# A gated mix of a long convolution and a shift MLP: the convolution in one piece, and in two channel chunks

## The chip, the cores and the metric

The kernel runs on one core of a Trainium2 chip. The metric is the device time of one execution in microseconds (us), lower is better. The core has five engines with an instruction queue each: PE multiplies matrices (PEld is its weight load), DVE and ACT do elementwise work and are the only ones that read PE's results out of PSUM, POOL does small elementwise work, and SP only issues transfers. SP, ACT and POOL each have a DMA queue; all of them share 16 DMA engines.

## The reference

The input is a sequence of S = 2048 rows with D = 640 channels, all in bf16. Two branches read it and a gate mixes them.

```
def _A_ref(q, k, v, shift_k, ssm_k, ssm_D):        # branch A: convolution over the sequence
    k_shift[s] = sum over t of k[s - t] * shift_k[:, t]        # 4 taps per channel
    kv = k_shift * v
    y  = causal convolution of kv with ssm_k, per channel, 2048 taps (by FFT), + kv * ssm_D
    return q * y

def _B_ref(x, w1, w2, w3, w4):                     # branch B: mixer
    h  = gelu(layernorm(x) @ w1)                   # 640 x 640
    hs = (four channel groups of h, shifted by 1, -1, 2, -2 rows) @ w2
    x1 = x + hs
    return x1 + gelu(layernorm(x1) @ w3) @ w4      # 640 x 1536, 1536 x 640

g = sigmoid((x * gate_w).sum(-1)) ; out = g * a + (1 - g) * b      # x is A_q
```

## The kernel before, in words

The sequence is laid out as 128 partitions x 16 row tiles of 640 channels; tile u holds rows 16p + u. Four tiles make a group. Q holds A_q and is later overwritten with branch B's sums.

**Branch B.** `norm_stats` takes means and variances on DVE, and 1/sqrt on POOL; `norm_apply` normalizes on DVE (xn, L329), transposes on PE (L336) and copies the transposed block XNT out of PSUM on ACT. `first_product` (L370) gives gelu(.. @ w1) into GS with the shift; `second_product` (L452) adds .. @ w2 to Q; `third_product` (L466) gives gelu(.. @ w3) into three tiles G; `fourth_product` (L479) adds .. @ w4. `US` is the order of the four tile groups in the later products.

**Branch A.** `short_conv` (L431) does the four taps on DVE: eleven elementwise operations for a group of four tiles. The long convolution is a transform in two steps. `step1` (L286) multiplies the filter's rows, then the signal's, by F1, copies the result AR out of PSUM on ACT and writes it to DRAM (SH, SX). `spectrum` (L563) goes over 32 frequency tiles t: `spec_h` reads SH back as BH, multiplies by M2 and copies to HS on ACT, and swaps the two halves of HS by two DMAs per pair of t on SP's queue; `spec_x` does the same for SX and multiplies with both forms of HS on DVE into XPB; `spec_z` multiplies by G1 and G2, copies ZG out (ACT and DVE in turn) and writes it to DRAM (SZ). `y_group` (L591) reads SZ back as ZT, multiplies by F1T, scales by the gate (ty), multiplies by q and adds branch B. The gate itself is `gate_dot` and `gate_act` on DVE and ACT; `scale_b` multiplies branch B's tile by 1 - g on ACT. `filter_transpose` (L308) turns the filter rows HN on PE and stores them as HTA (12 tiles, copied by DVE) and HTB (4 tiles, by ACT). Tables M2, G1, G2, F1 and F1T are made at the start from integers on POOL, DVE and ACT (`pbits`, `affine`, `wrap`, `sines`); `masked_blocks` spreads them into masked copies, six on ACT and six on DVE.

**Buffers.** Tiles with one tag share a ring of buffers, and a new tile waits until the oldest use of a buffer is over.

```
def big(name, ...):     tag="b5",  bufs=11      # L75: KT VT acc tmp CJ KHALO AR HTB BH BX HS ZG ZT, 5 KB each
def weights(...):       tag="w",   bufs=3       # L84: W12, GEN, HTA, W3, W4, XPB
load_h:                 tag="g",   bufs=3       # L112: HN, and later G of third_product
XNT and load_cjr's CJR: tag="xnt", bufs=2       # L325, L405
ps_tile:                tags "pc" and "pm", two PSUM buffers each
```

**Order.** Up to `front.__exit__` the engines' order is written out by hand (from the constants to the last part of `first_product(3, ..)`, with `filter_transpose` 0 to 4 and the first steps of `short_conv(0)` in between). After it a scheduler orders the instructions by the order of the program text and by when it thinks they are ready. That order is made by generators: `merge(a, b, ratio)` steps b by ratio times the cost that a yields. `conv_front` (the short convolution with step 1 of filter and signal) is merged with `mixer` at 1.0, `spectrum` with the rest of `mixer` at 1.5; then come the third product of the last group, `y_group` 3 and 0, and the last fourth product merged with `y_group` 1 and 2. The spectrum can start only when step 1 of all signal groups is done, since BX reads rows of all of them. Engines issue in order: an instruction that waits holds up those behind it in its queue, and a DMA on SP's queue does so too.

Of the kernel before, what the change touches and what calls it, by code (L numbers as in the profile page):

```python
# [10 lines left out]
ALU = mybir.AluOpType  # L11
# [6 lines left out]
def kernel(  # L18
# [32 lines left out]
    assert S == 2048 and P == 128 and D % P == 0 and Fh % (4 * P) == 0  # L51
# [7 lines left out]
    shifts = [1, -1, 2, -2]  # L59

# [14 lines left out]
    def big(name, shape=None, dtype=BF16):  # L75
        return main.tile(shape or [P, 4, D], dtype, name=name, tag="b5", bufs=11)
# [18 lines left out]
    def halves(ap):  # L95
        return ap.rearrange("p (h d) -> p h d", d=HD)

# [25 lines left out]
    load_h(0)  # L123
# [12 lines left out]
    def load_w2():  # L136
# [6 lines left out]
    ET = mybir.EngineType  # L143
    front = tc.manual_schedule(engines={ET.PE, ET.DVE, ET.Activation, ET.Pool})
    front.__enter__()
    IDB = consts.tile([P, P], BF16, name="IDB")
    nc.gpsimd.memset(IDB[:], 0.0)
    nc.gpsimd.affine_select(out=IDB[:], in_=IDB[:], compare_op=ALU.not_equal, fill=1.0,
                            base=0, pattern=[[-1, P]], channel_multiplier=1)
# [5 lines left out]
    def pbits(mask, mul, add, name):  # L155
        ti = consts.tile([P, 1], I32, name=name + "i")
        nc.vector.tensor_scalar(out=ti[:], in0=pidx[:], scalar1=mask, scalar2=None, op0=ALU.bitwise_and)
        tf = consts.tile([P, 1], F32, name=name)
        nc.vector.tensor_scalar(out=tf[:], in0=ti[:], scalar1=float(mul), scalar2=float(add),
                                op0=ALU.mult, op1=ALU.add)  # L160
        return tf

    pf = consts.tile([P, 1], F32, name="pf")
    nc.vector.tensor_copy(out=pf[:], in_=pidx[:])

    pf4 = pbits(31, 16, 1, "pf4")
    pfi = pbits(96, 0.125, 0, "pfi")
    nc.vector.tensor_tensor(out=pf4[:], in0=pf4[:], in1=pfi[:], op=ALU.add)

    GENW = main.tile([P, 3, 1024], I32, name="GEN", tag="w", bufs=3)  # L170


    def norm_stats(src):
        mv = small.tile([P, 4, 2], F32, name="mv")
        for i in range(4):
            st = small.tile([P, 2, 6], F32, name="st")
            for h in range(2):
                nc.vector.bn_stats(out=st[:, h, :], in_=src[i][:, h * HD:(h + 1) * HD])  # L178
            nc.vector.bn_aggr(out=mv[:, i, :], in_=st[:])
        ve = small.tile([P, 4], F32, name="ve")  # L180
        nc.gpsimd.tensor_scalar(out=ve[:], in0=mv[:, :, 1], scalar1=1e-5, scalar2=None, op0=ALU.add)
        rs = small.tile([P, 4], F32, name="rs")
        nc.gpsimd.tensor_tensor(out=rs[:], in0=ve[:], in1=NH[:], op=ALU.pow)
        return mv, rs
# [3 lines left out]


    F1 = consts.tile([P, 2, P], BF16, name="F1")  # L190
    F1T = consts.tile([P, 2, P], BF16, name="F1T")
    for gi, (dst, col_mul, col_add, prow) in enumerate(((F1, 4, 1, pf), (F1T, 1, 0, pf4))):
        t1 = main.tile([P, 320], I32, name="GENF", tag="r", bufs=6)
        t2 = main.tile([P, 320], I32, name="GENF", tag="r", bufs=6)
        ic = t1[:, 0:P]
        nc.gpsimd.iota(ic, pattern=[[col_mul, P]], base=col_add, channel_multiplier=0)
        jj = t2[:, 0:2 * P].rearrange("p (c k) -> p c k", c=2)
        for comp, off in ((0, 384.0), (1, 0.0)):
            nc.vector.tensor_scalar(out=jj[:, comp, :], in0=ic, scalar1=prow[:], scalar2=off,
                                    op0=ALU.mult, op1=ALU.add)  # L200
        last_f = nc.vector.tensor_scalar(out=jj, in0=jj, scalar1=511, scalar2=None, op0=ALU.bitwise_and)
        nc.scalar.activation(out=dst[:], in_=jj, func=ACT.Sin, bias=NPI[:], scale=2 * PI_ / 512)
# [7 lines left out]
    GA, GB, GC = GENW[:, 0, :], GENW[:, 1, :], GENW[:, 2, :]  # L210
    icf, ick, icn, m1 = GA[:, 0:512], GA[:, 512:1024], GB[:, 0:512], GB[:, 512:1024].bitcast(F32)
    nc.gpsimd.iota(icf.rearrange("p (g i n) -> p g i n", i=4, n=16), pattern=[[64, 8], [4, 4], [512, 16]],
                   base=0, channel_multiplier=0)
    nc.gpsimd.iota(ick.rearrange("p (g i n) -> p g i n", i=4, n=16), pattern=[[64, 8], [4, 4], [0, 16]],
                   base=0, channel_multiplier=0)
    nc.gpsimd.iota(icn.rearrange("p (m n) -> p m n", n=16), pattern=[[0, KH], [1, 16]],
                   base=0, channel_multiplier=0)
    midp = pbits(120, 0.125, 0, "midp")
    basep = pbits(3, 16, 1, "basep")
    offp = [pbits(4, -512, 6144 + 2048 * ro, f"offp{ro}") for ro in range(2)]  # L220
    for ro in range(2):
        nc.vector.scalar_tensor_tensor(out=offp[ro][:], in0=basep[:], scalar=midp[:], in1=offp[ro][:],
                                       op0=ALU.mult, op1=ALU.add)
    basei = pbits(15, 512, 1, "basei")
    kli = pbits(48, 0.0625, 0, "kli")
    nc.vector.scalar_tensor_tensor(out=basei[:], in0=kli[:], scalar=16.0, in1=basei[:], op0=ALU.mult, op1=ALU.add)
    offi = [pbits(64, -64, 6144 - 2048 * o, f"offi{o}") for o in range(2)]
    off2 = consts.tile([P, 1], F32, name="off2")
    nc.vector.memset(off2[:], 6144.0)
# [13 lines left out]

    for ro in range(2):
        affine(GC[:, 512 * ro:512 * ro + 512], icf, midp[:], offp[ro][:])
    st0 = norm_stats(tiles_of(range(4)))
    nc.vector.scalar_tensor_tensor(out=m1, in0=ick, scalar=basei[:], in1=icn, op0=ALU.add, op1=ALU.mult)
    wrap(GC)
    for o in range(2):
        affine(GA[:, 512 * o:512 * o + 512], m1, 1.0, offi[o][:])  # L250
    sines(M2, GC, True)
    for o in range(2):
        affine(GC[:, 512 * o:512 * o + 512], m1, 1.0, (0.0, off2[:])[o])
    klf = pbits(3, 1, 0, "klf")
    MK = []
    for name, kl in (("f", klf), ("i", kli)):
        mk = consts.tile([P, 4], F32, name="mk" + name)
        MK.append(mk)

    def masks():  # L260
        for mk, kl in zip(MK, (klf, kli)):
            for j in range(4):
                nc.vector.tensor_scalar(out=mk[:, j:j + 1], in0=kl[:], scalar1=float(j), scalar2=None,
                                        op0=ALU.is_equal)

    def masked_blocks():
        n = 0
        for dst, mk, inner in ((M2, MK[0], True), (G1, MK[1], False), (G2, MK[1], False)):
            for j in range(4):
# [9 lines left out]
                yield 0.0  # L279


    SH = dram.tile([32, P, D], BF16, name="SH")
    SX = dram.tile([32, P, D], BF16, name="SX")
    SZ = dram.tile([4, 32, 32, D], BF16, name="SZ")

    def step1(src, dst_dram, g):  # L286

        for hf in range(2):
            AR = big("AR", [P, 2, 2, D])
            for n in range(2):  # L290
                for h in range(2):
                    c0 = (2 * hf + n) * D + h * HD
                    ps = ps_tile("ps1", "pc")
                    for comp in range(2):
                        nc.tensor.matmul(ps[:, comp, 0:HD], lhsT=F1[:, comp, :], rhs=src[:, c0:c0 + HD],  # L295
                                         start=True, stop=True)
                    evac("a", AR[:, n, :, h * HD:(h + 1) * HD], ps[:, :, 0:HD])
                    yield 0.27
            r0 = 8 * g + 4 * hf
            nc.scalar.dma_start(out=bass.AP(tensor=dst_dram.tensor, offset=dst_dram[r0, 0, 0].offset,  # L300
                                            ap=[[D, P], [P * D, 4], [1, D]]),
                                in_=AR[:].rearrange("p n r d -> p (n r) d"))


    HT, HTA = [], []
    held = {}

    def filter_transpose(dt):  # L308
        if not HT:
            hta = weights("HTA", [P, 12, D])  # L310
            HTA.append(hta)
            HT.extend([hta[:, 4 * g:4 * g + 4] for g in range(3)] + [big("HTB")[:]])
        pst = psum.tile([P, N2, P], BF16, name="psh", tag="pc")
        hv = HN[dt].rearrange("p (n m) -> p n m", m=N2)
        for n2 in range(N2):
            nc.tensor.transpose(out=pst[:, n2, :], in_=hv[:, :, n2], identity=IDB[:])
        held["v"] = evac("v", HTA[0][:, :, dt * P:(dt + 1) * P], pst[:, 0:12, :])
        held["a"] = evac("a", HT[3][:, :, dt * P:(dt + 1) * P], pst[:, 12:16, :])
        if dt == DT - 1:
            nc.vector.tensor_tensor(out=HT[0][0:1, 0, :], in0=HT[0][0:1, 0, :], in1=DROW[0:1, :], op=ALU.add)  # L320
# [497 lines left out]
```

## Time and profile before

| what | value |
|---|---|
| median of 3 runs | 314.17 us (311.94 to 315.86) |
| the profiled execution, its own time | 313.56 us |
| its span in the profile | 311.8 us |
| mean granted TensorE clock | 0.949 |
| instructions | 4270 |
| DMA | 59.59 MB in 28,087 packets, 191 GB/s mean |
| DMA engines' busy share by queue | SP 37.7%, ACT 15.9%, POOL 3.5% |

The profile is of one execution. Busy time is the sum of an engine's instructions; a wait is put down to what came last before the waiting instruction could start; the chain follows the end of the execution back from step to step. L numbers are lines of the kernel. "DMA X<-Y" as a releaser is a transfer from Y to X. A line such as L90 is that of a helper (`evac` on ACT; L93 the same on DVE), so its tiles' names tell what it is.

### The profile page before, as it was taken

The page shows a single profiled execution, that of the slowest core. Times are in us where ns is not written, and L with a number is a line of the kernel's source. Part 1 is how long each engine was busy: PE and PEld are TensorE (multiplying, and loading weights), DVE is VectorE, ACT ScalarE, POOL GpSimd, SP SyncE. Part 2 cuts the span into 40 slices and gives each one's busy share as a digit, 9 for nine tenths or more (in the row PEclk, how much of TensorE's full clock was granted, in tenths as well). Part 3 has the DMA queues.
Part 4 walks back from the last instruction along what each step waited for, and adds up shares of the span by engine and source line. Part 5 has one row for each costly group of instructions (what it writes and reads, how often), then busy time and mean ns, then how long its engine had stood idle before and what let it go on. Part 6 is the DMA issues. An engine that isn't in the chain of part 4 may idle for free.

```text
span 311.8 us, 4270 instructions
## 1 busy us (share of the span) xinstructions
PE 246.6 (79%) x1572; PEld 148.1 (48%) x1572; DVE 198.5 (64%) x411; ACT 186.7 (60%) x265; POOL 38.1 (12%) x72
## 2 busy tenths in 40 slices
PE   0266729795986972899999883999998997599994
PEld 0223406563642440466447552665555664345673
DVE  8887805299985910499908893799443565601982
ACT  4493432426986686283685271467889799546740
POOL 4555450225010000000000320000000000000000
PEclk9997969999996998699999997899999999999999
DMA  7992771000275259442844797668774945269741
GB/s 227 396 254 103 253 321 67 2 17 6 86 247 205 93 188 373 159 170 84 273 149 133 215 326 253 211 192 225 261 229 140 291 146 161 89 220 371 263 182 63
DMA packets 28087, 59.59 MB, mean 191 GB/s; under 512 B 2051, under 2 KB 19203, under 8 KB 28066
## 3 DMA queue, kind: packets, MB, share of 16 engines
q1 hardware_dynamic: 13042, 38.18, 37.7%
q10 hardware_dynamic: 14224, 17.70, 15.9%
q0 software_dynamic: 800, 3.44, 3.5%
q8 instruction: 12, 0.20, 0.3%
q14 instruction: 9, 0.07, 0.1%
HBM read 35.71 MB, written 18.35 MB: 173 GB/s over the span
## 4 chain that ended last, share of the span: by engine, by line
PE 53%; DVE 22%; DMA 10%; ACT 8%; POOL 3%; issue 3%; SPq 0%; ACTq 0%; POOLq 0%; DVEq 0%
PE psw L479 16%; PE psw L466 14%; DVE st L178 5%; PE psz L542 5%; DMA W<-in_B_w_dram 4%; PE psw L452 4%; DMA BX<-SX 4%; PE psw L370 3%; ACT XNT L90 3%; PE psy L603 3%; PE ps L295 3%; PE psx L526 2%; DVE acc L441 2%; DVE tmp L439 2%; PE psh L513 2%
## 5 line engine op out<-in xcount | busy, mean ns | idle before, releaser
L479 PE MATMUL psw<-W,G 128*128 128x320 bf16 x384 | 64.7, 308 | 8.3 <-DMA W<-in_B_w_dram 6.4
L466 PE MATMUL psw<-XNT,W 128*128 128x512 bf16 x240 | 60.6, 387 | 0.2 <-ACT G L363 0.2
L90 ACT CAST AR<-ps 128x640 bf16<-128x640 f32 x64 | 41.5, 701 | 25.5 <-PE ps L295 20.1
L479 PEld LDWEIGHTS <-G 128*128 128x128 bf16 x384 | 38.6, 101 | 25.2 <-DMA W<-in_B_w_dram 6.8
L531 DVE TENSOR_TENSOR XPB<-XPB,HS 128x640 bf16<-128x640 bf16 x64 | 28.3, 487 | 21.3 <-ACT XPB L90 21.3
L466 PEld LDWEIGHTS <-W 128*128 128x128 bf16 x240 | 23.9, 99 | 24.0 <-issue 2.2
L363 ACT ACTIVATE G<-psw 128x1024 bf16<-128x1024 f32 x24 | 24.9, 1038 | 11.0 <-PE psw L466 10.9
L91 ACT ACTIVATE HS<-psh 128x640 bf16<-128x640 f32 x32 | 22.8, 719 | 13.1 <-PE psh L513 13.1
L370 PE MATMUL psw<-XNT,W 128*128 128x512 bf16 x80 | 21.7, 425 | 10.5 <-ACT XNT L90 9.6
L336 PE MATMUL pst<-IDB,xn 128*128 128x128 bf16 x160 | 13.6, 231 | 18.2 <-POOL GS L348 13.8
L90 ACT CAST XPB<-psx 128x640 bf16<-128x640 f32 x32 | 22.6, 707 | 8.9 <-PE psx L526 8.8
L542 PE MATMUL psz<-XPB,G 128*128 128x320 bf16 x128 | 23.6, 303 | 5.0 <-DVE ZG L93 1.6
L90 ACT COPY XNT<-pst 128x2048 bf16<-128x2048 bf16 (+1 forms) x16 | 19.3, 1240 | 13.6 <-PE pst L336 7.1
L178 DVE BATCH_NORM_STATS2 st<-Q 128x6 f32<-128x320 bf16 x64 | 27.3, 466 | 0.1
L452 PE MATMUL psw<-W,GS 128*128 128x320 bf16 x160 | 23.8, 299 | 4.1 <-ACT XNT L90 2.9
L455 DVE TENSOR_TENSOR Q<-psw,Q 128x640 bf16<-128x640 f32 x16 | 12.8, 806 | 14.5 <-PE psw L452 14.5
L295 PEld LDWEIGHTS <-F 128*128 128x128 bf16 x128 | 12.5, 98 | 19.4 <-issue 12.5
L336 PEld LDWEIGHTS <-xn 128*128 128x128 bf16 x160 | 11.0, 103 | 21.6 <-DVE xn L329 17.8
L452 PEld LDWEIGHTS <-GS 128*128 128x128 bf16 x160 | 15.6, 98 | 10.8 <-issue 4.8
L370 PEld LDWEIGHTS <-W 128*128 128x128 bf16 x80 | 8.7, 108 | 22.0 <-issue 15.2
L526 PE MATMUL psx<-BX,M 128*128 128x320 bf16 x64 | 14.5, 308 | 5.8 <-DMA BX<-SX 4.9
L542 PEld LDWEIGHTS <-G 128*128 128x128 bf16 x128 | 12.4, 98 | 13.8 <-issue 6.9
(113 smaller groups left out, 344.3 us busy)
## 6 DMA issues: line engine op xcount, KB each, us to landing
SH<-AR ACTq DMA_DIRECT2D x8, 640.0 KB, 3.6
SX<-AR ACTq DMA_DIRECT2D x8, 640.0 KB, 3.3
BH<-SH SPq DMA_DIRECT2D x8, 640.0 KB, 4.3
HS<-HS SPq DMA_DIRECT2D x32, 160.0 KB, 2.9
BX<-SX SPq DMA_DIRECT2D x8, 640.0 KB, 4.4
SZ<-ZG ACTq DMA_DIRECT2D x8, 640.0 KB, 3.4
ZT<-SZ SPq DMA_DIRECT2D x8, 640.0 KB, 6.2
HN<-in_A_ssm_k_dram SPq DMA_DIRECT2D x5, 512.0 KB, 10.9
```

The source lines that it names most:

```text
L90: return nc.scalar.copy(out=o, in_=i)
L91: return nc.scalar.activation(out=o, in_=i, func=ACT.Copy, scale=scale)
L178: nc.vector.bn_stats(out=st[:, h, :], in_=src[i][:, h * HD:(h + 1) * HD])
L295: nc.tensor.matmul(ps[:, comp, 0:HD], lhsT=F1[:, comp, :], rhs=src[:, c0:c0 + HD], start=True, stop=True)
L336: nc.tensor.transpose(out=pst[:, dd, i * P:(i + 1) * P], in_=xns[i][:, (d0 + dd) * P:(d0 + dd + 1) * P], identity=IDB[:])
L363: nc.scalar.activation(out=o, in_=i, func=ACT.Gelu_apprx_tanh)
L370: nc.tensor.matmul(ps[:, j, :], lhsT=w1_cols(dt, nt), rhs=XNT[:, dt, :], start=(dt == 0), stop=(dt == DT - 1))
L452: nc.tensor.matmul(ps[:, h, 0:HD], lhsT=GS[:, nt, u, :], rhs=W2P[:, nt, h * HD:(h + 1) * HD], start=(nt == 0), stop=(nt == DT - 1))
L466: nc.tensor.matmul(ps[:, j, :], lhsT=W3[:, dt, (f + j) * P:(f + j + 1) * P], rhs=XNT[:, dt, :], start=(dt == 0), stop=(dt == DT - 1))
L479: nc.tensor.matmul(ps[:, h, 0:HD], lhsT=G[ft // 4][:, ft % 4, i * P:(i + 1) * P], rhs=W4[0][:, ft, h * HD:(h + 1) * HD], start=(ft == 0), ...
L531: nc.vector.tensor_tensor(out=xp[:, 1 + a, :], in0=xp[:, 0, :], in1=HS[t // 2][:, a, t % 2, :], op=ALU.mult)
L542: mm = nc.tensor.matmul(pz[:, h, 0:HD], lhsT=gm[:, t].rearrange("p a b c -> p (a b c)"), rhs=XP[t][:, 1 + a, h * HD:(h + 1) * HD], start=( ...
```

## The change

The long and the short convolution are done in two chunks of channels, c = 0 with 384 and c = 1 with 256; all of KT, VT, KHALO, CJ, AR, BH, BX, HS, ZG, ZT and the DRAM buffers SH, SX, SZ exist per chunk. `big` becomes `chunk`, 18 buffers of 3 KB. `CJR` moves from the "xnt" ring into it, and taps are loaded and split per chunk. The spectrum's loop goes over 16 pairs m of frequency tiles: one PSUM tile holds both tiles of a pair, the product with both forms of HS is one DVE instruction on a tile PQ of the chunk ring, and XPB is gone. Two pairs of `spec_h` run ahead (before, five single tiles).

The order is now: `conv_a` (chunk 0: short convolution, step 1) with the mixer at 1.1; `spectrum(0)` with `conv_b` (chunk 1) at 2.2 and the mixer at 3.0; `spectrum(1)` with `mixer_end` at 1.4, which is the fourth product of US[2] and the y groups of chunk 0; then the third product of the last group, y of chunk 1 for groups 3 and 0, and the last fourth product with y of chunk 1 for groups 1 and 2. The 16 gate dots are woven into the fourth product of US[1] and the third of US[2], and every `scale_b` is issued in `y_group`.

In the front, the constants are made by three DVE operations on a row of eleven columns that POOL fills with memsets, instead of two operations per constant; GEN lies in the "g" ring as three tiles, so all loads of HN come after the sines; F1T is made after the sines; the memset of KHALO goes from POOL to DVE; `bn_aggr` is issued one tile later than its `bn_stats`; only three filter transposes and the first two steps of chunk 0's `short_conv(0, 0)` are in it. Transfers of K, V and the output are by chunk: 768 or 512 bytes per row and tile.

The diff, cut to its core:

```diff
-    def big(name, shape=None, dtype=BF16):
-        return main.tile(shape or [P, 4, D], dtype, name=name, tag="b5", bufs=11)
+    CH = [(0, DA * P), (DA * P, D - DA * P)]
+    def chunk(name, shape):
+        return main.tile(shape, BF16, name=name, tag="b3", bufs=18)
+    def pair(name, w):
+        return main.tile([P, 2, w], BF16, name=name, tag="xs", bufs=3)
...
+    def weave(lead, *others):
+        owed = [0.0] * len(others)
+        for c_ in lead:
+            yield c_
+            for n, (g_, speed) in enumerate(others):
+                owed[n] += c_ * speed
+                while owed[n] > 0:
+                    got = next(g_, None)
+                    if got is None:
+                        break
+                    owed[n] -= got
...
-    GENW = main.tile([P, 3, 1024], I32, name="GEN", tag="w", bufs=3)
+    GEN = [main.tile([P, 1024], I32, name="GEN", tag="g", bufs=3) for _ in range(3)]
...
+    const_row(cm[:, 0, :], cmask)
+    const_row(ca[:, 0, :], cmul)
+    const_row(ca[:, 1, :], cadd)
...
+    def step1(src, dst, g, w):
+        for hf in range(2):
+            AR = chunk("AR", [P, 2, 2, w])
+            for n in range(2):
+                ps = ps_tile("ps1", "pc")
+                for comp in range(2):
+                    nc.tensor.matmul(ps[:, comp, 0:w], lhsT=F1[:, comp, :], rhs=src(2 * hf + n),
+                                     start=True, stop=True)
+                evac("a", AR[:, n, :, :], ps[:, :, 0:w])
...
-        cjr = main.tile([P, D, 4], BF16, name="CJR", tag="xnt", bufs=2)
-        nc.gpsimd.dma_start(out=cjr[:], in_=A_shift_k.partition_broadcast(P))
+        cjr = chunk("CJR", [P, w, 4])
+        nc.gpsimd.dma_start(out=cjr[:], in_=A_shift_k[c0:c0 + w, :].partition_broadcast(P))
+        cj = chunk("CJ", [P, 4, w])
...
-        nc.gpsimd.memset(t[0:1, :, :], 0.0)
+        t = chunk("KHALO", [P, 3, w])
+        nc.vector.memset(t[0:1, :, :], 0.0)
...
+    def spec_x(c, m):
+        w = CH[c][1]
+        ps = forward(BX[c, m // 2], m, w)
+        xs = pair("XS", w)
+        evac("a", xs[:], ps[:, :, 0:w])
+        pq = chunk("PQ", [P, 2, 2 * w])
+        nc.vector.tensor_tensor(out=pq[:], in0=xs[:].rearrange("p t d -> p (t d)").unsqueeze(1).to_broadcast([P, 2, 2 * w]),
+                                in1=HS[c, m][:].rearrange("p a t d -> p a (t d)"), op=ALU.mult)
...
+    def spectrum(c):
...
+        for m in range(AH):
+            spec_h(c, m)
+            yield 0.33 * u
+        spec_x(c, 0)
+        yield 0.33 * u
+        for m in range(NM):
...
+            if m + AH < NM:
+                spec_h(c, m + AH)
+            if m + 1 < NM:
+                spec_x(c, m + 1)
+            yield 0.66 * u
+            spec_z(c, m)
+            yield 0.66 * u
...
+    def conv_b():
+        w = CH[1][1]
+        load_h(3)
+        load_h(4)
+        cjr = load_cj(1)
+        split_cj(1, cjr)
+        load_halo(1)
+        load_kv(1, 0)
+        load_kv(1, 1)
+        filter_transpose(3)
+        yield 1.0
+        filter_transpose(4)
+        yield 1.0
...
-    merge(conv_front(rows), mix, 1.0)
-    XPB.append(weights("XPB", [P, 4, 3, D]))
-    merge(spectrum(), mix, 1.5)
-    run(mix)
+    mix, conv = mixer(), conv_b()
+    run(weave(conv_a(), [mix, 1.1]))
+    run(weave(spectrum(0), [conv, 2.2], [mix, 3.0]))
+    run(conv, mix)
+    def mixer_end():
+        ya = chain(*[y_group(0, g) for g in range(NG)])
+        for i, u in enumerate(US[2]):
+            with tc.issue_after(LAST[-1].ins):
+                run(fourth_product([u], G_[2], False, i))
+            yield 3.2
+            for _ in range(2 if i < 3 else 1):
+                yield next(ya)
+        yield from ya
+    mix = mixer_end()
+    run(weave(spectrum(1), [mix, 1.4]))
+    run(mix)
     with tc.issue_after(LAST[-1].ins):
         run(third_product(Ys[0], G_[3]))
-    early = set(US[3])
-    run(y_group(3, early), y_group(0, early))
-    merge(fourth_product(US[3], G_[3], True), chain(y_group(1, early), y_group(2, early)), 0.6)
+    run(*[y_group(1, g) for g in (3, 0)])
+    run(weave(fourth_product(US[3], G_[3], True), [chain(y_group(1, 1), y_group(1, 2)), 0.6]))
```

## The prediction

> **What bounds the kernel now.** I read the page first, then busy time by stretch, then the chain that ended last, then the waits and the forms of the instructions.
>
> ```profile
> PE 246.6 (79%) x1572; PEld 148.1 (48%) x1572; DVE 198.5 (64%) x411; ACT 186.7 (60%) x265; POOL 38.1 (12%) x72
> ```
> ```profile
> 0.00:78.40 78.40, 45.82 (x326) 27.21 (x327) 53.52 (x148) 36.58 (x53) 31.86 (x62) 0.93 0.49 164
> 78.40:272.30 193.90, 165.35 (x1027) 99.63 (x1027) 127.43 (x228) 131.58 (x190) 6.28 (x10) 0.95 0.61 197
> 272.30:311.80 39.50, 35.39 (x221) 21.30 (x218) 17.57 (x37) 18.57 (x23) 0.00 (x0) 0.98 0.59 217
> ```
> The columns are PE, PEld, DVE, ACT and POOL busy, granted clock, DMA share, GB/s. The cuts are mine: 78.4 is where the second product of US[1] starts on PE, 272.3 where the spectrum ends. No engine is full: the front waits on a chain through all engines, the middle has PE at 85% with DVE and ACT at 66% and 68%, and only the tail is PE's own.
>
> The chain, in order of time (start, length, what):
> ```profile
> 40.35 2.78 POOL CJ L412 x4
> 43.16 1.88 ACT XNT L90
> ...
> 91.78 4.42 DMA SH<-AR
> ...
> 114.17 11.67 DMA W<-in_B_w_dram
> ...
> 182.29 11.20 DMA BX<-SX
> ...
> 272.32 12.95 PE psw L466 x60
> ```
> The waits (total, times, longest):
> ```profile
> DVE acc L438 <- DMA SH<-AR: 17.2, 1, 17.2
> ...
> ACT XNT L90 <- POOL CJ L412: 6.4, 1, 6.4
> ...
> PE psw L479 <- DMA W<-in_B_w_dram: 6.4, 1, 6.4
> ```
> X2's XNT sits in a two-slot ring, one slot of which CJR holds until POOL has split it. The short convolution of group 1 stops 17.2 us because AR holds the slots of the 11-buffer ring that acc needs. W4 waits for HTA's slot.
>
> One instruction shows a neighbour's cost (timeline, start and length):
> ```profile
> 21.75 1.69 POOL L419 MEMSET KHALO<- 1x1920 bf16 x1
> 21.83 3.33 DVE L329 TENSOR_SCALAR xn<-Q,mv,rs 128x640 bf16<-128x640 bf16 x4 [1.12 <-POOL rs L183]
> ...
> 33.29 1.51 DVE L329 TENSOR_SCALAR xn<-Q,mv,rs 128x640 bf16<-128x640 bf16 x4
> ```
>
> **Prices.** PE at full clock: 12.95/60 = 0.216 us for 512 columns and, from the tail's 6.53 us for 48, 0.136 for 320; so 0.163 for 384 and 0.109 for 256. ACT out of PSUM has rows of 0.384 (256 columns), 0.490 (384), 0.600 (512), 0.70 (640), 1.04 (1024); 768 is 0.81 between the last two. DVE on bf16: 1.49 us for 2560 elements, 28.3/64 = 0.44 for 640, so 0.09 plus 0.55 ns each. DVE out of PSUM: 0.82 for 640.
>
> **Front (78.4 us).** CJR leaves XNT's ring: ACT's 6.4 us go. What is late next is st3's rs, ready at 40.35, whose user X3 starts only at 53.2, so I take all of it (ends 5 and 6.4). KHALO's memset moves from POOL to DVE: four xn cost 1.8 us less; the memset on one partition costs DVE between 0.06 (the NPI memset) and 1.69 (this one on POOL); nearer DVE's own row, 0.4: gain 1.4. From 62.3 to 81 the chain is DVE's work. Two of three HTA copies leave it (1.9 us), the DROW add narrows by 0.3, and the nine conv0 pieces there, 9.4 us, become 0.81 + 0.6 × 8.6 = 6.0 at 384 of 640 columns, 3.4 less: 5.6 (ends 3, if PE's first product binds instead, and 8). The tables: 2.5 us of small DVE instructions ahead of st0 shrink, but three wraps and F1T's matrix (2.1 + 1.2 us) now stand ahead of st1: zero (ends -2.7 and +2). POOL's 27 memsets are hidden by the wait for Q and st0; without that cover they cost at most 27 × 0.1 = 2.7. HN's loads move behind the sines, since GEN holds their ring, SP's W2 goes ahead of them, and the first transpose is at 31: zero, up to 3. Front: 78.4 - 6.4 - 1.4 - 5.6 = 65.0.
>
> **Middle.** The matmul columns stay the same; fixed costs shift a little. It now has three stages, and I sum each engine in each.
>
> *A, first chunk's convolution beside the mixer.* Its lead costs of about 31, times 1.1, reach half of fourth_product(US[0]). ACT: 32 AR × 0.81 = 25.9, 6 gelu 6.2, two XNT 5.0, six masked blocks 7.0: 44.1. DVE: one group is 32 × 384 × 0.55 ns + 11 × 0.09 = 7.8 us, 3.63 groups are left: 28.3; with stats 4.2, xn 3.6, adds 4.8, masks 2.8: 43.7. PE: 5.4 + 13.0 + 10.4 + 2.6 + 6.5 = 37.9. ACT leads. ACT's fullest 20 us before had 17.43 busy (87%): 44.1/0.87 = 50.7. Eighteen smaller buffers leave ten for AR beside the eight of the convolution, where there were two: the 17.2 us wait should go. W4's slot comes free after 16 AR instead of 32, so W4 should land as the third product ends: zero (ends 0 and 11.7).
>
> *B, spectrum of the first chunk, convolution of the second, the mixer's rest.* PE: fourth 6.5 + 13, second 10.8, third 26, transposes 4.9, step 1 64 × 0.109 = 7.0, spectrum 128 × 0.163 = 20.9: 89.1. DVE: four groups of 5.5 = 22, 16 products of 1536 elements at 0.93 = 14.9, gate 12.6, adds 11, ZG 7.8, stats 8.4, xn 3.6, HTB 2: 82. ACT: 26.2 + 6.6 + 19.2 + 12.5 + 5 + 1.6 = 71. PE leads as from 200 to 260 before, where it was busy 58.44 of 60 (97%): 91.9. XPB's wait for W12 goes, and nothing replaces it. A wait is added: HN 3 and 4 need slots that G_[0] holds until the fourth product of US[0] ends, and behind them on SP stand the second chunk's halo and K, V loads, the next HS swaps and BX; spec_x's product waits for those. Zero if the scheduler puts the swaps first, else up to 11.2, the length of BX's worst landing. At B's start BX reads what A's last AR wrote, 3.3 + 4.4 us by their rows; ready mixer work covers it, else it costs 7.7.
>
> *C, spectrum of the second chunk, fourth_product(US[2]), y of the first.* ACT: HS and XS 32 × 0.60 = 19.2, ZG 4.8, 16 ty × 0.49 = 7.8, 16 scale_b × 0.854 = 13.7: 45.5. PE: 14 + 13 + 5.2 = 32. DVE 29. ACT leads; the 13.7 of scale_b wait for almost nothing and fill gaps, so 0.95: 47.9.
>
> **Tail.** Third 13.0, fourth 13.0, y of 256 columns 32 × 0.109 = 3.5, so 30 for the 35.3 that PE took (272.3 to 307.6); 4.2 to the end as before.
>
> Sum: 65.0 + 50.7 + 91.9 + 47.9 + 30 + 4.2 = 289.7 of span; the execution's time was 1.8 above its span (313.56 to 311.8): 291.5, against 313.56. The median of the runs shown, 314.17, is 0.6 above that execution, well inside their spread.
>
> **Queues.** SP issues 64 HS swaps for 32 at 0.56 us each, and twice the BH, BX, ZT, K, V reads: some 70 us of SP in 290, hidden as long as a swap is issued within C's 3 us per pair (two swaps, and half of a BH and BX each, take 1.7); without that cover each pair runs later by what is over.
>
> **Packets, a price the trace lacks.** Rows of 1280 B become 768 and 512, K and V lose their 5120 B runs: SH, SX, SZ 12,288 more packets, ZT 4,096, K and V 7,168, BH, BX and HS 4,096, together 27,600. Below end: nothing, since the SP queue's packets (2927 B mean) took 37.7% of 16 × 311.8 us for 38.18 MB, 49 us of engine time per MB, and ACT's (1244 B) 15.9% for 17.70 MB, 45, no dearer when smaller. Above: every packet costs ACT's mean of 56 ns whatever its size, 27,600 × 56/16 = 97 us of all engines. I take zero, by the two rows.
>
> SH<-AR landed its 640 KB in 3.6 us. The Trainium skill (DMA: Bandwidth & Descriptors, Anatomy of one DMA, fitted there for POOL's queue) has 2.0 us fixed plus bytes over 436 GB/s, 3.5 us for that, and its Rules for kernel authors ask for 1 MiB per DMA, which speaks against this change. By it a hand-off in chunks pays 2.0 us more wherever one is waited for; at the start of each spectrum that would be 4 us, and the sum 295.5.
>
> **Rivals.** *PE all through.* If the three stages blend, only PE's columns count: (37.9 + 89.1 + 32)/0.97 = 164, and 65 + 164 + 34.2 + 1.8 = 265. For it: PE, DVE and ACT totals of the middle are alike (159, 155, 161), so an even mix could do it. Against it: ACT leads at both ends by data order.
>
> *The waits only move.* The middle stays at 85% of its leading engine: (44.1 + 89.1 + 45.5)/0.85 = 210, 311 in all. For it: 18 slots serve two convolution chunks and a spectrum at once (some 13 + 9), and SP is one queue.
>
> *Slower: DMA becomes the bound.* The middle's DMA share, 0.61 of 193.9, is 118 us. With 85 of the 97 us above added it is 203; at the fullest share seen (0.92, first 20 us) that is 221 and 322 in all. It decides once a further packet costs over some 50 ns; the two queue rows speak against it.
>
> **How the numbers follow.** Forecast (281 to 305) 0.56; PE all through (265 to 281) 0.19; waits only move (305 to 316) 0.16; DMA bound (over 320) 0.09. Two per cent, about what a measurement can tell from no change, is 307.9 to 320.5. Faster: 0.56 + 0.19 + 0.04 of the third = 0.79; slower 0.09; same 0.12. The range is 272 to 311: it leaves out the last case, 0.05 above it and 0.06 below. The forecast's own is 281 to 305.
>
> **What would show it.** No ACT wait on CJ and PE's second product of US[1] near 65; no long DVE wait on SH<-AR; no PE wait on W over 2 us; spectrum's first ZG products before 130 with conv work beside them on DVE; PE busy over 92% from 116 to 208; ACT the fullest engine after that; DMA share under 0.75. Wrong if the front ends after 70, if the DMA share passes 0.85, or if spec_x waits on swaps.

## The result and the profile after

The changed kernel takes 348.72 us (median of 4 runs, 346.68 to 350.62), the kernel before 314.75 (4 runs beside them): 1.109 times as long, interval 1.100 to 1.119. Where a ratio is given below, disturbed executions are left out of it, so that it can differ from the quotient of two medians.

Busy time of the engines after:

```profile
PE 267.9 (77%) x1572; PEld 154.1 (44%) x1572; DVE 199.9 (57%) x410; ACT 190.3 (55%) x281; POOL 38.2 (11%) x103
```

The same 1572 matmuls take PE 21 us longer than the 246.6 before; the mean granted clock fell from 0.949 to 0.87. DVE and ACT have the work they had. So the loss is waiting, and a slower PE between the waits.

The stages by the forecast's own cuts (length, then PE, PEld, DVE, ACT and POOL busy, granted clock, DMA share, GB/s): front, A, B, C, tail.

```profile
0.00:70.20 70.20, 46.16 (x298) 26.34 (x299) 49.47 (x135) 39.43 (x55) 29.39 (x88) 0.91 0.49 163
70.20:118.30 48.10, 43.64 (x250) 24.59 (x250) 34.94 (x59) 31.95 (x40) 3.35 (x7) 0.93 0.61 197
118.30:230.50 112.20, 95.44 (x583) 55.35 (x582) 78.24 (x154) 69.21 (x99) 5.42 (x8) 0.94 0.69 200
230.50:313.40 82.90, 51.30 (x258) 29.33 (x257) 27.54 (x44) 36.69 (x65) 0.00 (x0) 0.69 0.51 150
313.40:348.80 35.40, 31.34 (x189) 18.51 (x186) 9.70 (x21) 13.00 (x23) 0.00 (x0) 0.93 0.33 108
```

Against the forecast (65.0, 50.7, 91.9, 47.9, 34.2) that is +5.2, -2.6, +20.3, +35.0, +1.2. More than half of the miss is C, the second chunk's spectrum with y of the first chunk beside it. There no engine is full, and the clock is 0.69.

The chain that ended last, in B and C (start, length, what):

```profile
162.79 10.18 DMA SH<-AR
...
242.01 4.97 DMA ZT<-SZ
251.57 4.95 PE psw L555 x24
262.85 3.96 DMA ZT<-SZ
273.22 4.37 PE psw L555 x24
283.99 3.77 DMA ZT<-SZ
...
301.98 3.38 DMA ZT<-SZ
```

C repeats rounds of some 20 us: a read of ZT, y, after the first three reads a burst of 24 matmuls of the fourth product (3.27 us at full clock, the first two here 4.4 to 5), three pairs or more of the spectrum, the next read. The waits (total, times, longest) say that PE itself stands at those reads:

```profile
PE psy L674 <- DMA ZT<-SZ: 15.7, 5, 4.2
...
ACT HS L97 <- DMA SH<-AR: 7.0, 1, 7.0
```

One round on SP's queue and then on PE (timelines):

```profile
238.86 2.42 SPq L596 DMA_DIRECT2D HS<-HS  x4
241.39 1.03 SPq L666 DMA_DIRECT2D ZT<-SZ  x2
```
```profile
245.33 0.50 PE L674 MATMUL psy<-ZT,F1T 128*128 128x384 bf16 x1 [4.16 <-DMA ZT<-SZ]
245.63 0.64 PE L585 MATMUL psf<-BH,M 128*128 128x256 bf16 x2
```

SP issues the reads of ZT behind four swaps and just before their use; PE has psy next in its queue and waits 4.16 us; the spectrum's psf stands behind psy, so the spectrum waits as well. The clock is 0.50 from 242 to 250, and the burst of 24 matmuls at 251.37 takes 5.15 us. But it had fallen before PE began to wait, at 241.2 (2 us each, columns as above):

```profile
236.00:238.00 2.00, 0.73 (x6) 0.48 (x5) 0.74 (x2) 2.00 (x4) 0.00 (x0) 0.95 0.37 79
238.00:240.00 2.00, 1.00 (x4) 0.38 (x4) 1.24 (x2) 2.00 (x4) 0.00 (x0) 0.50 0.77 249
```

The Trainium skill (TensorE: Matmul & The Clock Gate, HAM oscillation — how this bites in real kernels) says that an idle gap of more than some 3.4 us halves PE's clock, to be paid again in each round of a loop. The clock does halve in each round here, but in the first three before the long wait begins (by 238, 262 and 282.5; the waits begin at 241.2, 263.6 and 283.6), behind gaps of at most 1.3 us. So the wait for ZT is not what lowers it first, and the rule does not cover these rows; a run below shows the same without any long wait.

### The profile page after: what moved, and what is told of

Read it like the earlier page. It is cut to its first block, busy times and chain, and to the rows that moved or that the text cites. A ratio compares the mean times of both kernels' runs of the same rounds, so it can differ in the third digit from the quotient of the medians.

```text
span 348.8 us, 4509 instructions
## 1 busy us (share of the span) xinstructions
PE 267.9 (77%) x1572; PEld 154.1 (44%) x1572; DVE 199.9 (57%) x410; ACT 190.3 (55%) x281; POOL 38.2 (11%) x103
## 4 chain that ended last, share of the span: by engine, by line
PE 48%; DVE 15%; DMA 14%; ACT 14%; issue 4%; SPq 2%; POOL 1%; ACTq 1%; DVEq 0%; POOLq 0%
PE psw L555 12%; PE psw L535 11%; PE psw L519 5%; DMA ZT<-SZ 5%; PE psw L428 4%; PE psy L674 4%; PE ps L357 4%; ACT XNT L96 4%; PE psz L620 3%; ACT HS L97 3%; DMA SH<-AR 3%; DVE st L210 3%; DMA W<-in_B_w_dram 2%; PE psf L585 2%; DMA HS<-HS 2%
## 5 line engine op out<-in xcount | busy, mean ns | idle before, releaser
L96 ACT CAST AR<-ps 128x768 bf16<-128x768 f32 (+1 forms) x64 | 42.1, 700 | 26.6 <-PE ps L357 25.1
L604 DVE TENSOR_TENSOR PQ<-XS,HS 128x1536 bf16<-128x1536 bf16 (+1 forms) x32 | 26.3, 823 | 31.1 <-ACT XS L96 16.5
L97 ACT ACTIVATE HS<-psf 128x768 bf16<-128x768 f32 (+1 forms) x32 | 22.8, 711 | 32.5 <-PE psf L585 20.9
L535 PEld LDWEIGHTS <-W 128*128 128x128 bf16 x240 | 24.2, 101 | 26.5 <-issue 5.3
L620 PE MATMUL psz<-PQ,G 128*128 128x384 bf16 (+1 forms) x128 | 28.3, 352 | 9.0 <-ACT HS L97 5.4
L674 PE MATMUL psy<-ZT,F1T 128*128 128x384 bf16 (+1 forms) x64 | 16.9, 392 | 18.4 <-DMA ZT<-SZ 15.7
L210 DVE BATCH_NORM_STATS2 st<-Q 128x6 f32<-128x320 bf16 x64 | 27.2, 470 | 1.2 <-DMA Q<-in_A_q_dram 1.0
L585 PE MATMUL psf<-BX,M 128*128 128x384 bf16 (+1 forms) x64 | 15.8, 330 | 14.9 <-DMA BX<-SX 5.0
L96 ACT CAST XS<-psf 128x768 bf16<-128x768 f32 (+1 forms) x32 | 22.2, 694 | 6.6 <-PE psf L585 6.3
L97 ACT ACTIVATE ty<-psy,G 128x384 bf16<-128x384 f32 (+1 forms) x32 | 14.8, 525 | 18.4 <-PE psy L674 17.6
L585 PEld LDWEIGHTS <-M 128*128 128x128 bf16 x128 | 12.5, 102 | 27.6 <-issue 16.1
L620 PEld LDWEIGHTS <-G 128*128 128x128 bf16 x128 | 14.3, 112 | 20.2 <-issue 12.0
```

The source lines that it names most:

```text
L96: return nc.scalar.copy(out=o, in_=i)
L97: return nc.scalar.activation(out=o, in_=i, func=ACT.Copy, scale=scale)
L535: nc.tensor.matmul(ps[:, j, :], lhsT=W3[0][:, dt, (f + j) * P:(f + j + 1) * P], rhs=XNT[:, dt, :], start=(dt == 0), stop=(dt == DT - 1))
L585: nc.tensor.matmul(ps[:, tt, 0:w], lhsT=M2[:, t].rearrange("p a b c -> p (a b c)"), rhs=src[:, t % 4, :], start=True, stop=True)
L604: nc.vector.tensor_tensor(out=pq[:], in0=xs[:].rearrange("p t d -> p (t d)").unsqueeze(1).to_broadcast([P, 2, 2 * w]), in1=HS[c, m][:].rea ...
L620: mm = nc.tensor.matmul(pz[:, tt, 0:w], lhsT=gm[:, t].rearrange("p a b c -> p (a b c)"), rhs=PQ[c, m][:, a, tt * w:(tt + 1) * w], start=(a ...
```

## The experiments

All times are device us, beside the kernel before on the same chip (313.5 to 314.4). "Span" is that of a profiled execution (some 1.8 below its time). The runs on C were executed once each, and the four executions of the changed kernel lie 4 us apart. C is taken from the end of the first spectrum's last product on PE, at 230.5 in the changed kernel and at 226.7 to 232.0 in these runs, to the third product of the last group.

### y of the first chunk behind the second spectrum

```diff
-        ya = chain(*[y_group(0, g) for g in range(NG)])
         for i, u in enumerate(US[2]):
...
-            for _ in range(2 if i < 3 else 1):
-                yield next(ya)
-        yield from ya
...
     run(mix)
+    run(*[y_group(0, g) for g in range(NG)])
```

> The y groups of the first chunk stand behind the second spectrum; only the four fourth products stay beside it. Theory Y (PE waits in order for ZT reads that SP issues just before their use, and the spectrum behind them stops too): the stage of the second spectrum falls from 82.9 us to 50 to 58, y of the first chunk costs 12 to 20 after it, total 328 to 342. Theory loop (the second spectrum is slow by itself: HS, swap, product, two PSUM buffers): the stage stays at 70 or more, total 355 or more.

Measured 319.32, 29.4 less than the change and below both ranges, and C takes 48.1 us:

```profile
228.84:277.00 48.16, 35.65 (x227) 22.92 (x225) 19.49 (x29) 28.52 (x49) 0.00 (x0) 0.87 0.63 178
```

So y beside the second spectrum cost that stage 34.8 us, nearly the whole of the 35.0 that C missed; behind it, between matmuls of the third product, it costs some 5 (the rest of the span is 40.6 for 35.4).

### The second spectrum alone

```diff
-    run(weave(spectrum(1), [mix, 1.4]))
+    run(spectrum(1))
```

> The second spectrum runs with nothing woven into it; the fourth products and y of the first chunk follow it. Theory loop: the 16 pairs by themselves take 55 us or more. Theory Y: they take 28 to 38 (some 2 us a pair, as between two ZT waits), and the rest, 13 of fourth products and y with its ZT waits, 30 to 40 more, so the total is near that of the changed kernel, 340 to 352.

Measured 328.75. The 16 pairs take 44.5 us, between the two theories:

```profile
228.86:273.40 44.54, 31.90 (x130) 16.26 (x129) 16.26 (x24) 26.30 (x45) 0.00 (x0) 0.50 0.68 195
```

That is 2.7 us from one pair's psz to the next with nothing beside it, so the chain of small steps (HS, swap, product, Z) has a pace of its own, worth 44.5 of the 47.9 us that I gave to the whole stage. With the four fourth products beside it (the run before this one) it takes 48.1: they cost 3.6 and not 13. PE runs at half clock here all the time, though its longest gap in that stretch is 1.6 us, and the half clock may be a part of this pace: at full clock, three pairs in a row with no large product between them took 6.1 us in the run before (psz from 259.07 to 265.19), 2.0 each, but in the changed kernel 2.4 and 2.7 (psz at 257.42, 260.13, 262.53). How much of the 44.5 us is the slow PE, between nothing and some 10 us by these rows, no run separates.

### The reads of ZT one group ahead, on three queues

On SP's queue (each pair of reads one y group early, the first ahead of the second spectrum), then the same on POOL's queue, then on ACT's queue with each read right after the group before:

```diff
+        ZT = ZTS.pop((c, g), None) or load_zt(c, g)
+        if c == 0 and g + 1 < NG:
+            ZTS[c, g + 1] = load_zt(c, g + 1)
...
-            nc.sync.dma_start(out=zt[:], ...
+            nc.gpsimd.dma_start(out=zt[:], ...        # second run
+            nc.scalar.dma_start(out=zt[:], ...        # third run, c == 0
```

> Each pair of ZT reads of the first chunk is issued one y group earlier than its use, the first ahead of the second spectrum; everything else as changed. Theory Y: the four waits of 4 to 5 us for ZT go, and the granted clock in the stage rises above 0.75; the stage falls from 82.9 to 58 to 66, total 325 to 334. Theory loop: the pairs still take their time and less than 6 us go.

> As in the run with ZT read one group ahead (337.9 of span), but all ZT reads are issued on POOL's queue, which is empty then, so that a read that waits for its data or a buffer holds up no swap on SP. Theory order (reads stuck in SP's queue are the loss): the 12 us stop at the start of the second spectrum, where the early read stood ahead of BH, goes, and ZT waits stay gone: the stage from 230 to the third product's start takes 52 to 62, total 318 to 328. Theory clock (PE has gaps whatever the reads do, its clock falls to 0.5 to 0.75 and the stage is then half bound by a slow PE): total 332 to 340.

> The changed kernel with ZT of the first chunk read through ACT's queue, in line with ACT's work, from the second group on issued right after the group before; y stays beside the second spectrum. Theory order (reads and their burst were the loss): no read waits 4 us but the first, and there is no stop of 9 us on swaps at the start as with POOL's queue: the stage falls to 50 to 60, total 318 to 326. Theory clock and PE order (psy, psf and psz share two PSUM buffers and one queue with bursts of 24 matmuls, PE's gaps keep its clock low): stage 64 to 72, total 329 to 338.

Measured 339.68, 334.12 and 330.38, each above the range of the theory that the order of the reads was the loss; C takes 71.8, 71.2 and 67.3 us for 82.9. In the first, the early read of ZT, which could go out only at 235.95, stood in SP's queue ahead of BH, and PE stood 5.8 us. In the second, both groups' reads (1.5 MB) went out at once when the first spectrum ended (POOL's timeline), and the swaps issued beside them landed late (waits):

```profile
231.69 2.16 POOL L668 DMA_DIRECT2D ZT<-SZ  x4 [68.40 <-DVE Q L566]
```
```profile
DVE PQ L604 <- DMA HS<-HS: 23.1, 6, 9.6
```

The third has neither:

```profile
227.17:294.50 67.33, 44.07 (x259) 26.88 (x257) 27.27 (x45) 36.71 (x65) 0.00 (x0) 0.82 0.64 191
```

It gains 15.6 us in C: the same matmuls take PE 7.2 us less, at 0.82 of the clock for 0.69, and PE is idle 8.3 us less; its waits for ZT fell by 9.4 (6.3 left of 15.7, the first read alone 5.6). So some 16 of the 35 us that C missed are the reads' place. The rest stays: with y behind the spectrum C took 48.1, so y beside it still costs 19, of which its own 32 matmuls are 5.2 at full clock.

### PSUM buffers of y

On the last kernel, `ps_tile("psy", "pc")` becomes `ps_tile("psy", "pc" if c else "pm")`.

> On top of the run with ZT read through ACT's queue (328.6 of span): y of the first chunk takes its PSUM buffers from the ring of the products (pm), not from the one that the spectrum uses (pc). Theory PSUM (psy holds one of two buffers until ACT has copied it, and psf and psz of the spectrum wait for that): the stage falls from 64.0 to 52 to 58, total 318 to 324. Theory order (PE runs its queue in order, and each burst of 24 matmuls or of psy stops the chain HS, swap, product for its own length): 61 to 66, total 326 to 331.

Measured 332.84, C no shorter (69.3 us for 67.3). So two PSUM buffers that it need not share with y do not help the spectrum; psy now shares with the fourth products' psw, so that sharing is not ruled out altogether. What remains is the order on PE, which no run here proves by itself.

### Four pairs ahead

First with `AH = 4` alone in the changed kernel; later, on the version with y late and slower companions (below), for the second spectrum only, with BH and BX read one group earlier.

> Four pairs of spec_h run ahead instead of two, in both spectra. Theory loop: the waits of PQ for the swaps of HS (14.3 and 17.8 us of DVE and ACT waits) go and the stage of the second spectrum falls by 12 us or more. Theory Y: ZT waits stay, the stage changes by less than 5. In the first spectrum two more HS hold two more of the 18 buffers: it may lose up to 5.

> On top of the run with slower companions (314.3 of span): in the second spectrum alone four pairs of spec_h run ahead instead of two, with BH and BX read one group earlier, so that no read loses its lead as in the earlier run with four pairs (which read BH just before its use). Theory loop (the second spectrum waits for swaps and reads): its 16 pairs take 32 to 38 us for some 45, total 305 to 309. Rival (PE's order and clock pace it): within 3 us of 315.

The first took 379.06 and tests something else than I meant: spec_h then uses BH in the step that issues its read, and PE stops at eight of them:

```profile
PE psf L585 <- DMA BH<-SH: 31.1, 8, 6.7
```

The second, with lead, is 0.987 of before (0.981 to 0.992) against 1.005 without, 4.2 us of span; C takes 46.2 us for 48.6, in the two profiled executions. But all eight executions have a median of 315.19 (308.54 to 316.93), those without the lead 315.56 (313.51 to 318.42), so that the gain is not settled. If it holds, latency is a part of the pace, not the whole.

### Slower companions, and more work beside the spectra

```diff
-    run(weave(spectrum(0), [conv, 2.2], [mix, 3.0]))
+    run(weave(spectrum(0), [conv, 1.7], [mix, 2.3]))
```

on top of y late; then also the fourth product of US[2] at the end of `mixer`, and `third_product(Ys[0], G_[3])` woven into the second spectrum; then that with four pairs ahead.

> The kernel with y of the first chunk late, with the first spectrum's companions stepped more slowly (conv 1.7 for 2.2, mixer 2.3 for 3.0), so that they last until its end. Theory run-out (both ran out near 217, and the spectrum's last pairs and the first of the next ran alone to 240 with PE at 12.5 to 13 of 20 us): gain 3 to 8, total 311 to 316. Rival (the second chunk's rows come later, so that the second spectrum's start moves by as much): same or up to 5 slower.

> On top of the run with slower companions (314.3 of span): the fourth product of US[2] stands in the mixer beside the first spectrum's end, and the third product of the last group beside the second spectrum. Theory filler (each spectrum is a chain of small steps through memory, and PE idles in it unless large products stand beside it; the change leaves 13 us of them for the second): PE rises above 17 of 20 us in 200 to 280, total 303 to 310. Rival (the second spectrum paces itself at 2.3 to 2.9 us a pair, whatever stands beside it, and the moved products only leave a gap in the tail): 312 to 318.

> The chunk order with all that has helped: y of the first chunk late, slower companions, large products beside both spectra, four pairs ahead in the second. If the causes add: 311.3 less 4, so 305 to 309. Theory filler says more: what stands beside the spectra is a fixed stock of 39 us of third and fourth products, and two spectra in a row need it twice, so it stays 12 us or more above the 289.0 of the one-chunk kernel with twelve buffers. Rival (the chunk order is as good once its reads have lead): 290 to 300.

Measured 315.56 (1.005 of before, 1.000 to 1.009), 311.34 (0.990, 0.987 to 0.993) and 309.85 (0.992, 0.986 to 0.997). Each does a little, counted from the 319.32 of the single run with y late. In the last, PE is busy 18.0 to 20.0 of each 20 us from 180 to 240, and then runs out of large products (one line each 20 us):

```profile
240.00:260.00 20.00, 17.83 (x121) 11.37 (x119) 8.12 (x12) 14.18 (x24) 0.00 (x0) 1.00 0.75 211
260.00:280.00 20.00, 13.60 (x90) 8.27 (x87) 11.29 (x20) 12.62 (x24) 0.00 (x0) 1.00 0.79 240
280.00:300.00 20.00, 14.30 (x64) 8.02 (x65) 10.70 (x24) 8.40 (x20) 0.00 (x0) 0.57 0.68 226
```

The large products are a fixed stock, and what was moved beside one latency left a hole at another.

### XQ's loads in the first spectrum

On y late, the four loads go to SP's queue between swaps; and, on the version with slower companions, only the first of the four is left.

> The kernel with y of the first chunk late, with the four loads of XQ on SP's queue between HS swaps instead of all four at once on POOL's. Theory burst (2.6 MB of XQ at once hold up SH's last writes, which took 10.2 us for 256 KB at 162.8, and HS's allocation waits for their buffer): stretch 160 to 180, where PE had 13 of 20 us busy at clock 0.83, gains 4 to 7 us, total 311 to 315. Rival (the ring of 18 is full whatever XQ does): within 2 us of 319.

> On top of the run with slower companions (314.3 of span): only the first of the four loads of XQ is left, 0.65 of 2.6 MB, and the gate and y read its four tiles in place of all sixteen, so three quarters of q's values are replaced by others; the instructions are the same. Theory burst: stretch 160 to 180, where PE had 13.8 of 20 us, rises to 17 or more and the whole gains 4 to 7. Rival (18 buffers for a spectrum and a convolution chunk, whatever XQ does): PE stays under 15 there, gain under 2.

The first shows nothing: SP issued the loads all the same between 159 and 173 (DMA share 0.97 from 160 to 180), and its two runs, 316.63 and 321.79, are too far apart. The second, one execution, took 309.75, 6.3 us of span less than the profiled one with all loads; the first spectrum ends 6.3 us earlier (219.1 for 225.4). The stretch from 160 to 180, with all four loads and with one:

```profile
160.00:180.00 20.00, 13.82 (x78) 8.43 (x76) 14.62 (x34) 9.13 (x15) 2.27 (x4) 0.83 0.89 298
```
```profile
160.00:180.00 20.00, 17.21 (x113) 11.42 (x111) 19.66 (x44) 10.66 (x17) 0.00 (x0) 0.91 0.68 199
```

So 2.6 MB at once cost B some 6 us. It fits that transfers which others wait for landed sooner (SH's and SX's writes, at most 9.9 us to landing with all loads, 5.7 with one).

### Parts of the change, and one more buffer, in the kernel before

```diff
-        cjr = main.tile([P, D, 4], BF16, name="CJR", tag="xnt", bufs=2)
+        cjr = big("CJR", [P, D, 4])
...
-        nc.gpsimd.memset(t[0:1, :, :], 0.0)
+        nc.vector.memset(t[0:1, :, :], 0.0)
```

then also `bufs=12` for 11 in the ring of 5 KB buffers (and 3 for 4 in the ring of edge tiles, to pay for it), then `bufs=12` without the other two.

> The kernel before, with two parts of the change alone: CJR in the ring of big buffers, out of XNT's, and the memset of KHALO on DVE. My prediction's terms: 6.4 and 1.4 us off the front, 305.5 to 308, if nothing later takes them back. Rival (the front's chain meets another wait, or the big ring is short by one buffer): gain of 0 to 3, 311 to 314.

> The kernel before with CJR out of XNT's ring and KHALO's memset on DVE (302.0), and one more of the 5 KB buffers (12 for 11; the ring of edge tiles has 3 for 4 to pay for it). The DVE wait of 16.7 us on SH's write before acc should go, as my prediction had it for the change; if that stop is on the path (PE had 11.4 of 20 us busy in 100 to 120), total 294 to 299; if W4's landing ends last in that stretch, 299 to 303.

> The kernel before with twelve 5 KB buffers for eleven (edge ring 3 for 4) and nothing else; CJR stays in XNT's ring, KHALO's memset on POOL. If the two add: 314 less 13, 299 to 304. If the front's stop covers it (acc's wait comes later by what the front loses): 306 to 312.

Measured 302.02 (0.959 of before, 0.950 to 0.969), 289.01 (0.920, 0.915 to 0.925) and 299.11 (0.957, 0.949 to 0.966); the first two gained more than either of their ranges had it. The two gains add: 11.8 and 15.1 make 26.9, together they give 25.3. The second product of US[1] starts at 67.75 in the first of them, 78.41 before. What the twelfth buffer does, from 100 to 120, with eleven and with twelve (the first two runs):

```profile
100.00:120.00 20.00, 11.40 (x71) 6.48 (x69) 3.12 (x4) 11.13 (x17) 0.00 (x0) 0.74 0.75 262
```
```profile
100.00:120.00 20.00, 15.88 (x97) 9.34 (x96) 12.67 (x14) 16.53 (x24) 0.00 (x0) 0.91 0.81 286
```

DVE's wait before acc falls from 16.7 us (on SH's write) to 9.2 and 2.1, and its work there goes from 3.1 to 12.7 us. PE's wait for W4, 6.2 us with eleven buffers, is gone as well, so that the gain is not the short convolution's alone. At 289.0 us this one-chunk kernel is the fastest of all that ran, 8% below before, 21 us below the best in chunks; its PE is 84% busy.

## Why the prediction was wrong

**Step that failed: C, "ACT leads ... so 0.95: 47.9".** I divided the sum of the fullest engine by a share, 0.95, that no row gave: the stretches that I took for A and B had 0.87 on ACT and 0.97 on PE, with large products to fill them. Nothing led here: ACT had 36.7 us of work in 82.9. What the runs put in its place: the 16 pairs have their own pace (44.5 us alone, at half clock), and with the fourth products beside them they fill 48.1, the whole of what I gave; y was not hidden in that but cost 34.8 more. Some 16 of these are reads of ZT with no lead in a queue that serves the spectrum. The other 19 come with y between the spectrum's steps; that they are the order on PE's one queue is argued, not shown. The forecast's "hidden as long as a swap is issued within C's 3 us per pair" asked how long SP issues, not what it has in front of it and what PE has behind.

**B, "PE leads as from 200 to 260 before ... (97%)".** The sum of PE was right: 89.1 at full clock is 94.8 at the 0.94 granted, and 95.4 was measured. The share was 85%. XQ's burst is some 6 us of the 20.3 that B missed; the companions ended before the spectrum (slower ones gave 3.8, large products moved beside both spectra 4.2 more, not all of it in B). I had given no term to either, and some 6 to 10 us of B stay open.

**Front, 65.0 for 70.2.** CJR out of XNT's ring and the memset of KHALO were 7.8 in the forecast; alone, in the kernel before, they moved the second product of US[1] by 10.7, right in sign and too small. The 5.6 for DVE's chain from 62.3 to 81 failed: from the second half of US[0]'s second product to US[1]'s it took 21.8 us (48.47 to 70.22), 19.9 before. The pieces of the short convolution are shorter, but the statistics of US[0] now stand behind the third filter transpose. They start at 56.14, and in the kernel with only the two parts at 51.63 (chains):

```profile
53.50 1.01 PE psh L373 x16
...
56.14 1.58 DVE st L210 x4
```
```profile
50.80 0.83 DVE Q L455
51.63 0.80 DVE st L178 x2
```

I had counted what the edit shortens and not the step that it moves ahead.

**Right:** the acc wait of 17.2 and W4's wait gone; the tail (35.4 for 34.2). But most of the two waits needed no chunks to remove: in the kernel before, a twelfth buffer took W4's wait away and left 11.3 us of acc's.

**Right by luck:** A, 48.1 for 50.7. ACT was to lead it with 44.1 us of work; it had 31.95, and PE, with 37.9 at full clock forecast, was busy 43.64, 91% of the stage. The length came out, its reason did not.

**The signs.** Two of the three signs of being wrong came: the front ended after 70 (70.2), and the product PQ waited for swaps (14.3 us in 7 waits). The DMA share stayed under 0.85 in every stage (0.69 at most).

**The rivals.** "DMA becomes the bound" fell, with its price:

```profile
DMA packets 56291, 59.61 MB, mean 171 GB/s; under 512 B 3506, under 2 KB 47532, under 8 KB 56268
...
q1 hardware_dynamic: 28556, 38.18, 36.6%
q10 hardware_dynamic: 26896, 17.70, 15.9%
```

52.5% of 16 × 348.8 us is 2930 us of engine time for these two queues; 53.6% of 16 × 311.8 was 2674. The 256 us over 28,204 further packets are 9 ns each, near my zero and far from the 50 at which this rival decides. "The waits only move" came nearest in kind (SP is one queue) but had them cost 20 us, not 59. No rival of mine had what decided C: y between the steps of a spectrum that fills the stage by itself, with reads that have no lead in an ordered queue.

**The rule on small transfers.** SH's and BX's hand-offs take about as long in the smaller size, only ZT's is shorter (KB each, median us to landing; before, 640 KB took 3.6, 4.4 and 6.2):

```profile
SH<-AR ACTq DMA_DIRECT2D x8, 384.0 KB, 4.1
...
BX<-SX SPq DMA_DIRECT2D x8, 384.0 KB, 4.0
...
ZT<-SZ SPq DMA_DIRECT2D x8, 384.0 KB, 3.9
```

The Trainium skill (DMA: Bandwidth & Descriptors, Rules for kernel authors), with its 1 MiB per DMA, spoke against the change, and the direction came out so. But no run here changes the size of a transfer alone, a packet cost little, and at the same size other places for the reads gave 15.6 us in C. The forecast charged for two hand-offs by the page, 4 us, and none in the sum; what counts is how many are waited for, and there were four reads of ZT in C alone, at about 4 us each.

## What to carry to other kernels

Splitting a long dependent stage in two, as here, doubles its start, its end and its hand-offs, while the independent work to lay beside them stays the same: count that stock first, and give a stage of small steps its own measured pace, not a share of its fullest engine. For each read, ask what stands ahead of it in its queue, and what stands behind its user on PE. And try the single cause first: one more buffer, one tile in another ring and one memset on another engine gave here 25 us without the chunks.

## What the runs showed of the hardware that I had not expected

The second spectrum alone ran at a granted clock of 0.50 (for the 42.9 us from 230.5 on) with no gap on PE over 1.6 us: PE was idle 27% of the time (235 to 272: 27.2 busy of 37), in short gaps in every pair, and with the fourth products beside it the mean was 0.87. A rule of single gaps, as cited above, does not cover that. Beside four reads of 384 KB in one go, HS's swaps (64 KB each) took up to 6.2 us to land, with a median of 3.5 in that second spectrum, for 2.1 in the changed kernel's.
